# Attention, MLP and gate gradients on one core: dO sums one pair later, dwo and dw2 rows split between two engines, wide b and a products, four dV tiles stored in row pieces

## Chip, core and metric

The kernel runs on 1 core of one Trainium2 chip. The metric is device time in microseconds of one execution; lower is better. Three runs of the kernel before gave 405.79, 408.78 and 409.79 us (median 408.78).

## The reference

One decoding step of a gated mix of attention (A) and an MLP (B), and the gradients of all its inputs for a given `grad_out`. x has 640 elements, there are 32 heads of 128 with 4096 cached positions, and the MLP is 1728 wide. All tensors are bf16.

```python
def _A_ref(x, k_cache, v_cache, wq, wo):          # H, Dh = 32, 128
    q = (x @ wq).reshape(B, Sq, H, Dh).transpose(0, 2, 1, 3)
    scores = jnp.einsum("bhqd,bhkd->bhqk", q, k_cache) * (Dh ** -0.5)
    p = _softmax(scores, axis=-1)
    o = jnp.einsum("bhqk,bhkd->bhqd", p, v_cache)
    return o.transpose(0, 2, 1, 3).reshape(B, Sq, H * Dh) @ wo
def _B_ref(x, w1, b1, w2):
    h = jnp.einsum("bsd,df->bsf", x, w1) + b1
    sp = jnp.log1p(jnp.exp(-jnp.abs(h))) + jnp.where(h > 0, h, jnp.zeros_like(h))
    return jnp.einsum("bsf,fd->bsd", h * jnp.tanh(sp), w2)
g = _sigmoid((x * gate_w).sum(-1, keepdims=True))
out = g * _A_ref(...) + (1 - g) * _B_ref(...)
# returned: out and its gradients for A_x, A_k_cache, A_v_cache, A_wq, A_wo, B_w1, B_b1, B_w2, gate_w
```

The key and value caches are 33.6 MB each, and so are their gradients. With the weights and their gradients, 82.0 MB are read and 82.0 MB written.

## The kernel before, in words

The 32 heads go in 16 pairs. A pair's K or V is one tile of 128 partitions by 16 KB (2 MB): 64 partitions per head, 64 positions of 128 numbers in each. There are seven such buffers (`kv0` to `kv6`). A gradient tile is made in a buffer that its own K or V held, and stored from there, so a buffer comes free when its store has landed.

Each pair runs through 16 slots; (i, s) is slot s of pair i, and the order of all work is written out by hand. In slots 0 to 7 TensorE transposes V of pair i, in slots 8 to 15 K of pair i+1 (`transposes`, L368 to 376, with a ScalarE copy out of PSUM), and two slots later it forms dP or S from them (`products`, with 48 moving columns, W = 48, of which the first few count). The softmax is spread over slots 2 to 8 (`soft_max` to `soft_p`; `rz` is the reciprocal of its sum), o comes in slots 7 and 8, ds in 11, and the outer products dV in slots 9, 10, 12 and 13 and dK in slot 15 and in 0, 1 and 3 of the next pair (L463, 1.22 us each on VectorE).

Queues: loads are issued by SP, in the order of the list `loads` (L159 to 169). `pump` (L171) puts a load into SP's program as soon as that program has freed a buffer for it; SP then waits there until the store from that buffer has landed, and everything behind it on SP waits too. Stores of dV (slot 13) and dK (slot 3 of the next pair) are issued by POOL while loads remain, later by SP (L725 to 729, called at L757 and L776).

Heads also go in four groups of eight (g = 0 to 3, four pairs each). A group's rows of wo (1.3 MB) lie in `wob[g % 2]`, so groups 1 and 3 share a buffer, as do 0 and 2. What is done on it:

- `do_sum` (L287, VectorE, 8 per group): products of its rows with da, summed along the row: the gradient of o. It must be done before the group's first pair starts; `do_prep` builds dR, Dr and ndo from it in the slots behind.
- `a_cols` (L331, TensorE, 40 products per group with one moving column): the group's share of `a`.
- `dwo_row` (L352, ScalarE, 8 per group, 0.83 us each): overwrites the rows with the gradient of wo, behind `a_cols` and all the sums.
- `st_dwo` (L355, POOL) and, when it has landed, `ld_wo` (L156, SP) for the group two on.

For group g = 1 these stand at pair 8: `a_cols` in slots (8,2) to (8,4), `dwo_row` in (8,5) to (8,14), `st_dwo` at (9,0), `ld_wo(3)` at (9,1); `do_sum(3, 0)` stands at (10,6), `do_sum(3, 1)` at (10,14) and the other six at (11,5) to (11,7). Group 2's sums stand alike four pairs earlier, at (6,6), (6,14) and (7,5) to (7,7).

The MLP runs in pairs 0 to 6. Its w2 lies in 14 blocks of rows in columns of the wq tile: `mlp_b` (L566, TensorE, 70 products with one moving column, slots (1,14) to (2,2)) gives b, `mlp_dact` (L576, VectorE) reads the same blocks, and `mlp_dw2` (L581, ScalarE) overwrites them with the gradient of w2 in slots (2,3) to (3,6); `st_dw2` stores them at (3,9). `dx_sum` and `dwq_row` (L482, L487) do the like for wq, group by group.

Tables of the form `plan(i, {s: [(f, args)]})` and `at(i, s, f, args)` put such side work behind the main work of a slot (L647 to 703).

Of the kernel before, what the change touches and what calls it, by code (L numbers as in the profile page):

```python
# [9 lines left out]
ALU = mybir.AluOpType  # L10
AX = mybir.AxisListType
F32 = mybir.dt.float32
# [5 lines left out]
def kernel(  # L18
# [33 lines left out]
    nc = tc.nc  # L52
    P = 128
    _, H, Sk, Dh = A_k_cache.shape
# [5 lines left out]
    J = 64  # L60
    RC = D // P
# [4 lines left out]
    FN = FK + 1  # L66
    NBUF = 7
    NT = 4
    W = 48
# [32 lines left out]
    def C(shape, dt, name):  # L102
        return const.tile(shape, dt, name=name, tag=name)
# [3 lines left out]
    bufs = [big.tile([P, bufw.get(i, KVW)], BF16, name=f"kv{i}", tag=f"kv{i}") for i in range(NBUF)]  # L107
    wqa = big.tile([P, RC, H * Dh], BF16, name="wq", tag="wq")
    wob = [big.tile([P, 8, D], BF16, name=f"wo{i}", tag=f"wo{i}") for i in range(2)]
# [12 lines left out]
    kbuf, vbuf, mbuf = {}, {}, {}  # L122
# [48 lines left out]
    def pump():  # L171
        while loads and (free_q or not loads[0][0]):
            loads.popleft()[1]()
# [44 lines left out]
    mst = {}  # L218

    def misc(shape, dt, name):  # L220
        return one_ps.tile(shape, dt, name=name, tag="misc")
# [5 lines left out]
    db_bc = C([P, D], BF16, "db_bc")  # L227
    da_bc = C([P, D], BF16, "da_bc")
# [85 lines left out]
    a_acc = C([P, RC], F32, "a_acc")  # L314
    o8 = C([P, 8], BF16, "o8")
    o8f = C([P, 8], F32, "o8f")
# [13 lines left out]

    def a_cols(g, c0=0, c1=RC):  # L331
        if c0 == 0:
            mst["a"] = misc([P, RC], F32, "a_ps")
        ps = mst["a"]
        wv = wob[g % 2][:].rearrange("p k (n c) -> p k c n", c=RC)
        for c in range(c0, c1):
            for k in range(8):
                nc.tensor.matmul(ps[:, c:c + 1], lhsT=wv[:, k, c, :], rhs=o8[:, k:k + 1],  # L338
                                 start=(k == 0), stop=(k == 7))
        if c1 == RC:  # L340
            if g == 0:
                nc.vector.tensor_copy(a_acc[:], ps[:])
            else:
                nc.vector.tensor_tensor(a_acc[:], a_acc[:], ps[:], ALU.add)

    def scaled(eng, dst, src, col):
        if eng is nc.vector:
            nc.vector.tensor_scalar(dst, src, col, None, ALU.mult)
        else:
            nc.scalar.mul(dst, src, col)  # L350

    def dwo_row(g, k):  # L352
        nc.scalar.mul(wob[g % 2][:, k, :], da_bc[:], o8f[:, k:k + 1])  # L353

    def st_dwo(g, eng, k0=0, k1=8):  # L355
        eng.dma_start(dwo_v[g][:, k0:k1], wob[g % 2][:, k0:k1])
# [21 lines left out]
    def products(ps, src, c, col):  # L378
        for t in range(4):
            B = 4 * c + t  # L380
            for e in range(2):
                nc.tensor.matmul(ps[:, 4 * B:4 * B + W].rearrange("p (a b) -> p a b", b=4),  # L382
                                 lhsT=src[:, t, :, e],
                                 rhs=col[:, e, :, :].rearrange("p a b -> p (a b)").unsqueeze(1).to_broadcast([P, W // 4, 4]),
                                 start=(e == 0), stop=(e == 1))
# [116 lines left out]
    act_f = C([P, FN], F32, "act_f")  # L502
    act_b = C([P, FN], BF16, "act_b")
# [3 lines left out]
    b_acc = C([P, RC], F32, "b_acc")  # L507
# [5 lines left out]
    def w2row(k):  # L513
        n0 = HC + (k % 3) * D
        return wqa[0:P if k < FK else FR, k // 3, n0:n0 + D]

    def frange(k):
        return (P, slice(k, k + 1)) if k < FK else (FR, slice(FK, FN))
# [46 lines left out]

    def mlp_b(c0, c1):  # L566
        if c0 == 0:
            mst["b"] = misc([P, RC], F32, "b_ps")
        for c in range(c0, c1):
            for k in range(FN):  # L570
                n, ks = frange(k)
                nc.tensor.matmul(mst["b"][:, c:c + 1], lhsT=w2row(k).rearrange("p (n c) -> p c n", c=RC)[:, c, :], rhs=act_b[0:n, ks], start=(k == 0), stop=(k == FN - 1))
        if c1 == RC:
            nc.vector.tensor_copy(b_acc[:], mst["b"][:])

    def mlp_dact(k):  # L576
        n, ks = frange(k)
        nc.vector.scalar_tensor_tensor(junk[0:n, :], in0=w2row(k), scalar=1.0, in1=db_bc[0:n, :],  # L578
                                       op0=ALU.mult, op1=ALU.mult, accum_out=dact[0:n, ks])

    def mlp_dw2(k):  # L581
        n, ks = frange(k)
        nc.scalar.mul(w2row(k), db_bc[0:n, :], act_f[0:n, ks])

    def st_dw2():
        for t, v in w2_pieces:
# [30 lines left out]
    def at(i, s, f, *a):  # L617
        side.setdefault((i, s), []).append(lambda: f(*a))

    def plan(i, table):  # L620
        for s, tasks in table.items():
            for t in tasks:
                at(i, s, *t)

    def dx(g, part, c0, c1, *rcs):
        return [(dx_sum, g, part, c0, c1, rc) for rc in rcs]
# [4 lines left out]
    def rows(f, *ks):  # L631
        return [(f, k) for k in ks]

    def sums(g, *ks):
        return [(do_sum, g, k) for k in ks]

    def dwo(g, *ks):
        return [(dwo_row, g, k) for k in ks]

    def q_prep(i, s, g):  # L640
        plan(i, {s: [(q_half, g, 0)], s + 2: [(q_half, g, 1)], s + 3: [(q_dup, g)], s + 5: [(q_cols, g)]})

    def do_prep(i, s, g):
        plan(i, {s: [(do_hot, g)], s + 2: [(do_rows, g)], s + 3: [(do_dup, g)], s + 5: [(do_cols, g), (do_plain, g)]})
# [6 lines left out]
    for c, (i, s) in enumerate(((1, 14), (1, 15), (2, 0), (2, 1), (2, 2))):  # L651
        at(i, s, mlp_b, c, c + 1)
    plan(2, {5: rows(mlp_dact, 9, 10), 6: rows(mlp_dact, 11, 12), 7: rows(mlp_dact, 13), 14: sums(1, 0, 1)})
    q_prep(2, 8, 1)
    for k in range(FN):
        at(*((2, 3), (2, 4), (2, 6), (2, 7), (2, 9), (2, 10), (2, 12), (2, 13), (2, 14), (3, 1), (3, 2), (3, 3), (3, 4),
             (3, 6))[k], mlp_dw2, k)
    plan(3, {4: [(mlp_dh,)] + sums(1, 2), 5: sums(1, 3, 4), 6: sums(1, 5, 6), 7: sums(1, 7), 8: [(dh_hot, 0)],
             10: [(dh_row, 0)]})
    plan(3, {8: [(do_hot, 1)]})  # L660
    plan(3, {10: [(do_rows, 1)], 11: [(do_dup, 1)], 13: [(do_cols, 1), (do_plain, 1)], 14: [(dh_hot, 1)],
             15: [(o_dup, 0)]})
    plan(3, {9: [(st_dw2,)]})
    plan(4, {0: [(dh_row, 1)], 1: [(o_rows, 0)]})
    plan(4, {3: [(a_cols, 0, 0, 2)], 4: [(a_cols, 0, 2, 4)], 5: [(a_cols, 0, 4, 5)]})
    for k in range(8):
        at(4, (6, 7, 8, 9, 10, 12, 13, 14)[k], dwo_row, 0, k)
    plan(4, {5: rows(mlp_dxb, 0), 7: rows(mlp_dxb, 1), 14: rows(mlp_dxb, 2)})
    plan(5, {0: [(st_dwo, 0, nc.gpsimd)], 1: [(ld_wo, 2)], 5: rows(mlp_dxb, 3), 7: rows(mlp_dxb, 4), 14: dx(0, 0, 0, GC, 0)})
    plan(4, {10: [(ld_wq, HC, 2 * HC, nc.scalar)]})  # L670
# [2 lines left out]
    for g in range(NG - 1):  # L673
        i = 4 * g + 4
        if g:
            plan(i - 1, {14: [(o_dup, g)]})
            plan(i, {0: [(o_rows, g)], 2: [(a_cols, g, 0, 2)], 3: [(a_cols, g, 2, 4)], 4: [(a_cols, g, 4, 5)]})
            for k in range(8):
                at(i, (5, 6, 7, 9, 10, 12, 13, 14)[k], dwo_row, g, k)
            plan(i + 1, {0: [(st_dwo, g, nc.gpsimd)]})  # L680
            if g + 2 < NG:
                plan(i + 1, {1: [(ld_wo, g + 2)]})
        for k, (j, s) in enumerate((((1, 14), (2, 5), (2, 7), (3, 14), (3, 15)), ((1, 5), (1, 7), (2, 5), (2, 7), (2, 14)),
                                    ((0, 14), (1, 5), (1, 6), (1, 7), (1, 14)))[g]):
            if (g, k) != (0, 0):
                plan(i + j, {s: dx(g, g, 0, GC, k)})
            at(i + j, s + 1 if s < 15 else s, dwq_row, g, 0, GC, k)
    for g in (2, 3):
        i = 4 * g
        q_prep(i - 1, 2, g)  # L690
        plan(i - 2, {6: sums(g, 0), 14: sums(g, 1)})
        plan(i - 1, {5: sums(g, 2, 3), 6: sums(g, 4, 5), 7: sums(g, 6, 7)})
        do_prep(i - 1, 8, g)
    plan(12, {8: [(st_dwq, 0, HC, nc.scalar)]})
    plan(14, {6: [(st_dwq, HC, HC + GC, nc.gpsimd)]})
# [2 lines left out]
    g, i = NG - 1, NP - 2  # L698
# [14 lines left out]
    def run_products(i, s):  # L713
# [5 lines left out]
        else:  # L719
# [2 lines left out]
                S_ps[n] = one_ps.tile([P, 2 * J + W], F32, name="S", tag="S")  # L722
            products(S_ps[n], src, s - 8, qR[(n // 4) % 2][:, n % 4])

    def store_kv(dct, i, dst, eng):  # L725
        b = dct[i]
        eng.dma_start(dst, bufs[b][:, 0:J * Dh])  # L727
        free_q.append(b)
        pump()

# [3 lines left out]
    def slot(i, s):  # L734
# [16 lines left out]
        if chain_on:  # L751
            if s == 0:
                dq_row(i - 1)
            if s in (0, 1, 3):
                dk_quarter(i - 1, (0, 1, 3).index(s) + 1)
            if s == 3:
                store_kv(kbuf, i - 1, dKv[i - 1], nc.gpsimd if loads else nc.sync)  # L757
            if s == 2:
                soft_max(i)
            if s == 4:  # L760
                soft_maxt(i)
            if s == 7:
                soft_z(i)
# [9 lines left out]
        if s in (9, 10, 12, 13):  # L773
            outer(vbuf[i], st[i]["p"], Dr[(i // 4) % 2][:, i % 4, :], (9, 10, 12, 13).index(s))
            if s == 13:
                store_kv(vbuf, i, dVv[i], nc.gpsimd if loads else nc.sync)  # L776
# [73 lines left out]
    i, g = NP - 1, NG - 1  # L850
# [30 lines left out]
    dq_row(i)  # L881
    last_dv(1)
    a_cols(g)
    for k in range(8):
        dwo_row(g, k)
# [71 lines left out]
```

## Time and profile before

| What | us |
|---|---|
| three runs | 405.79, 408.78, 409.79 |
| span of the profiled execution, first to last instruction | 405.7 |
| busy: TensorE matmul / weight load | 299.9 / 275.3 |
| busy: VectorE / ScalarE / GpSimd | 279.1 / 259.9 / 25.1 |
| DMA: 164.88 MB, 15963 packets | mean 406 GB/s over the span |
| bytes read from and written to HBM | 82.03 MB and 82.03 MB |

The span is 0.1 us under the fastest run. How to read the rest of the profile: a row of instructions gives line, engine, operation, out<-in tiles and shapes, how many, busy time and the mean of one in ns, and the idle time of the engine ahead of them with what ended most of it. SPq, ACTq and POOLq are queues' own instructions (DMA issues and waits). The slices cut the span in 40 parts of 10.1 us, counted here from 0; a digit is a busy share in tenths, PEclk is the granted TensorE clock in tenths. From the DMA's issues: a 2 MB store by POOL landed 19.1 us after its issue at the median, a 2 MB load 18.8 to 18.9 us, a dwo store of 1.3 MB by POOL 26.2 us. The two forms of the products' rows: `b_ps` 70 with 128x1, first at 67.0 and last at 75.5 us; `a_ps` 160 with 128x1.

### The profile page before, as it was taken

To read this page: it belongs to the slowest core of one execution; us is meant where nothing else is said; L and a number is where in the kernel's file an instruction comes from. 1 tells how busy PE (TensorE), PEld (TensorE's weight loads), DVE (VectorE), ACT (ScalarE), POOL (GpSimd) and SP (SyncE) were. 2 spreads that over 40 slices of the span, in tenths; PEclk is the share of its full clock that TensorE was granted. 3 is DMA by queue.
4 is the path that set the end of the run, shared out by engine and by line. 5 is a ranking of instruction groups with operands and counts; after the bars stand their busy time and mean duration, and the time that the engine had idled before them with its cause. 6 is when DMAs were issued, how large, how long until landed. Compare 5 with 4: busy or idle time off the path is not lost.

```text
span 405.7 us, 13024 instructions
## 1 busy us (share of the span) xinstructions
PE 299.9 (74%) x5646; PEld 275.3 (68%) x5646; DVE 279.1 (69%) x596; ACT 259.9 (64%) x529; POOL 25.1 (6%) x50
## 2 busy tenths in 40 slices
PE   3769898998886887739979869704989998896210
PEld 3548898886775777729869769603889888886200
DVE  2744969489884968529795939306889598795850
ACT  3444545699857978617768976404676998986610
POOL 3000000002000101000000100000101010000020
PEclk9886999699999889857999999955999999999555
DMA  8999999999999999999999999999999999999993
GB/s 272 425 407 436 420 421 422 425 407 361 395 427 428 412 426 425 423 430 428 430 425 428 424 429 426 427 434 429 371 401 375 386 424 424 419 422 423 426 423 124
DMA packets 15963, 164.88 MB, mean 406 GB/s; under 512 B 1713, under 2 KB 1905, under 8 KB 6178
## 3 DMA queue, kind: packets, MB, share of 16 engines
q1 hardware_dynamic: 8832, 94.08, 55.9%
q0 software_dynamic: 5472, 63.42, 37.5%
q10 hardware_dynamic: 1602, 6.56, 4.0%
q8 instruction: 44, 0.72, 0.7%
q14 instruction: 13, 0.11, 0.1%
HBM read 82.03 MB, written 82.03 MB: 404 GB/s over the span
## 4 chain that ended last, share of the span: by engine, by line
issue 44%; DMA 22%; PE 13%; DVE 9%; ACT 4%; POOL 3%; SPq 0%; POOLq 0%; ACTq 0%; DVEq 0%
DMA kv<-in_A_k_cache_dram 11%; DMA out_dram<-wo 6%; DVE kv L463 5%; PE tr L372 5%; DMA wo<-in_A_wo_dram 5%; POOL out_dram L727 2%; ACT tch L375 2%; PE dq L431 2%; PE o L431 1%; PE dP L382 1%; PE S L382 1%; DVE wq L484 1%; ACT wq L350 1%; PE a_ps L338 1%; ACT wo L353 1%
## 5 line engine op out<-in xcount | busy, mean ns | idle before, releaser
L372 PE MATMUL tr<-idf,kv 128*128 128x128 f32 x1024 | 175.3, 298 | 13.6 <-DMA kv<-in_A_k_cache_dram 11.9
L375 ACT COPY tch<-tr 128x512 f32<-128x512 f32 x256 | 144.2, 586 | 57.1 <-PE tr L372 53.2
L372 PEld LDWEIGHTS tr<-idf,kv 128*128 128x128 f32 x1024 | 120.8, 153 | 19.7 <-issue 16.7
L382 PEld LDWEIGHTS <-tch 128*128 128x128 bf16 x2048 | 89.9, 100 | 57.4 <-ACT tch L375 52.5
L463 DVE TENSOR_TENSOR kv<-p_dup,Dr 128x2048 bf16<-128x2048 bf16 x64 | 76.6, 1220 | 5.5 <-ACT p_dup L422 5.2
L463 DVE TENSOR_TENSOR kv<-ds_dup,Qr 128x2048 bf16<-128x2048 bf16 x64 | 76.8, 1220 | 0.4
L382 PE MATMUL S<-qR,tch 128*128 128x48 bf16 x1024 | 48.4, 187 | 33.5 <-ACT tch L375 32.8
L431 PEld LDWEIGHTS <-kv 128*128 128x128 bf16 x2048 | 59.2, 97 | 4.6 <-issue 3.5
L382 PE MATMUL dP<-dR,tch 128*128 128x48 bf16 x1024 | 48.7, 187 | 10.6 <-ACT tch L375 10.0
L288 DVE SCALAR_TENSOR_TENSOR junk<-wo,da_bc 128x640 bf16<-128x640 bf16 x32 | 26.3, 822 | 33.2 <-DMA wo<-in_A_wo_dram 32.5
L431 PE MATMUL dq<-ds_m,kv 128*128 128x48 bf16 x1024 | 31.8, 184 | 4.1 <-DVE ds_m L453 2.5
L422 ACT ACTIVATE p_dup<-e_m,rz 64x128 bf16<-64x128 bf16 x32 | 12.7, 397 | 33.9 <-DVE rz L416 33.4
L727 POOL DMA_DIRECT2D out_dram<-kv x25 | 13.4, 536 | 296.5 <-DVE kv L463 244.4
L431 PE MATMUL o<-e_m,kv 128*128 128x48 bf16 x1024 | 31.6, 185 | 0.0
L353 ACT ACTIVATE wo<-da_bc,o8f 128x640 bf16<-128x640 bf16 x32 | 25.9, 826 | 1.6 <-PE a_ps L338 0.9
L350 ACT ACTIVATE wq<-dqrow,xf 128x1024 bf16<-128x1024 bf16 (+2 forms) x30 | 25.1, 860 | 1.4 <-DVE wq L484 1.0
L484 DVE SCALAR_TENSOR_TENSOR wq<-wq,dqrow 128x1024 bf16<-128x1024 bf16 (+2 forms) x30 | 25.1, 862 | 0.2
L437 DVE TENSOR_TENSOR o<-o,rz 128x2 f32<-128x2 f32 x16 | 2.5, 158 | 20.6 <-PE o L431 20.6
L404 DVE TENSOR_REDUCE negM<-mt 64x1 f32<-64x64 f32 x32 | 7.1, 222 | 11.4 <-PE mt L401 10.8
L457 ACT COPY ds_dup<-ds_m 64x128 bf16<-64x128 bf16 x32 | 9.5, 297 | 6.8 <-DVE ds_m L453 6.3
L409 ACT ACTIVATE e_m<-S,negM 64x64 bf16<-64x64 f32 x32 | 10.6, 331 | 4.5 <-DVE negM L404 4.0
L578 DVE SCALAR_TENSOR_TENSOR junk<-wq,db_bc 128x640 bf16<-128x640 bf16 (+1 forms) x14 | 11.5, 820 | 2.2 <-ACT db_bc L256 1.9
(159 smaller groups left out, 240.7 us busy)
## 6 DMA issues: line engine op xcount, KB each, us to landing
out_dram<-kv POOLq DMA_DIRECT2D x25, 2048.0 KB, 19.1
kv<-in_A_v_cache_dram SPq DMA_DIRECT2D x16, 2048.0 KB, 18.8
kv<-in_A_k_cache_dram SPq DMA_DIRECT2D x15, 2048.0 KB, 18.9
out_dram<-kv SPq DMA_DIRECT2D x5, 2048.0 KB, 25.5
wo<-in_A_wo_dram SPq DMA_DIRECT2D x4, 1280.0 KB, 19.8
out_dram<-kv SPq DMA_DIRECT2D x4, 1024.0 KB, 18.5
out_dram<-wo POOLq DMA_DIRECT2D x3, 1280.0 KB, 26.2
wq<-in_A_wq_dram SPq DMA_DIRECT2D x2, 1280.0 KB, 9.4
```

Source lines behind the costliest of these rows:

```text
L288: nc.vector.scalar_tensor_tensor(junk[:], in0=wob[g % 2][:, k, :], scalar=1.0, in1=da_bc[:], op0=ALU.mult, op1=ALU.mult, accum_out=do8[g % ...
L350: nc.scalar.mul(dst, src, col)
L353: nc.scalar.mul(wob[g % 2][:, k, :], da_bc[:], o8f[:, k:k + 1])
L372: nc.tensor.transpose(tp[:, t, :], src[:, 4 * c + t, :], idf[:])
L375: nc.scalar.copy(dst[:].rearrange("p a b e -> p (a b e)").bitcast(F32), tp[:].rearrange("p a b -> p (a b)"))
L382: nc.tensor.matmul(ps[:, 4 * B:4 * B + W].rearrange("p (a b) -> p a b", b=4), lhsT=src[:, t, :, e], rhs=col[:, e, :, :].rearrange("p a b - ...
L422: nc.scalar.activation(p[HS[hh]], e_m[i % 2][HS[hh], :, hh].unsqueeze(2).to_broadcast([64, J, 2]), ACT.Copy, scale=st[i]["rz"][HS[hh], hh: ...
L431: nc.tensor.matmul(st[i][key][:].rearrange("p (a b) -> p a b", b=2), lhsT=src[:, j, :], rhs=rhs[:, j, :].unsqueeze(1).to_broadcast([P, W / ...
L463: nc.vector.tensor_tensor(kview(b)[:, j0:j0 + n, :].rearrange("p j (a b) -> p j a b", b=2), col[:, j0:j0 + n, :].unsqueeze(2).to_broadcast ...
L484: nc.vector.scalar_tensor_tensor(w, in0=w, scalar=1.0, in1=dqrow[g % 2][:, c0:c1], op0=ALU.mult, op1=ALU.mult, accum_out=dq_acc[:, rc, par ...
L578: nc.vector.scalar_tensor_tensor(junk[0:n, :], in0=w2row(k), scalar=1.0, in1=db_bc[0:n, :], op0=ALU.mult, op1=ALU.mult, accum_out=dact[0:n ...
L727: eng.dma_start(dst, bufs[b][:, 0:J * Dh])
```

## The change

- The sums of groups 2 and 3 stand nine slots later for k = 0, at (6,15) and (10,15), and k = 1 at (7,4) and (11,4).
- `dwo_row` takes an engine. Group 1: all eight rows on VectorE in slots (8,5) and (8,6), its store at (8,7), the load of group 3's wo at (8,15). Group 0: four of the eight rows on VectorE. Groups 2 and 3: as before.
- `mlp_dw2` takes an engine: blocks 0 to 5 on VectorE at (2,3) and (2,4), 6 to 9 on ScalarE in (2,7) to (2,14), 10 to 13 on VectorE at (3,2). `st_dw2` stands at (3,4).
- The products of `mlp_b` and `a_cols` get 48 moving columns, copies of the one that counts; each overwrites the columns behind its own, which later products set anew.
- Two `dx_sum` and `dwq_row` of group 0 move from pair 7 to pair 6.
- The POOL stores of dV 3, 6, 9 and 12 are split by rows: 5+120+3, 14+105+9, 8+120 and 1+120+7, each piece a DMA of its own.

On VectorE the row is `tensor_scalar` by a column (`scaled`, L346, as it stands).

```diff
     def a_cols(g, c0=0, c1=RC):
         if c0 == 0:
-            mst["a"] = misc([P, RC], F32, "a_ps")
-        ps = mst["a"]
+            mst["a"] = misc([P, RC + W], F32, "a_ps")
+        ps = mst["a"][:, 0:RC]
...
-                nc.tensor.matmul(ps[:, c:c + 1], lhsT=wv[:, k, c, :], rhs=o8[:, k:k + 1],
+                nc.tensor.matmul(mst["a"][:, c:c + W], lhsT=wv[:, k, c, :], rhs=o8[:, k:k + 1].to_broadcast([P, W]),
                                  start=(k == 0), stop=(k == 7))
...
-    def dwo_row(g, k):
-        nc.scalar.mul(wob[g % 2][:, k, :], da_bc[:], o8f[:, k:k + 1])
+    def dwo_row(g, k, eng=nc.scalar):
+        scaled(eng, wob[g % 2][:, k, :], da_bc[:], o8f[:, k:k + 1])
...
-                nc.tensor.matmul(mst["b"][:, c:c + 1], lhsT=w2row(k).rearrange("p (n c) -> p c n", c=RC)[:, c, :], rhs=act_b[0:n, ks], start=(k == 0), stop=(k == FN - 1))
+                nc.tensor.matmul(mst["b"][:, c:c + W], lhsT=w2row(k).rearrange("p (n c) -> p c n", c=RC)[:, c, :],
+                                 rhs=act_b[0:n, ks].to_broadcast([n, W]), start=(k == 0), stop=(k == FN - 1))
...
-    def mlp_dw2(k):
+    def mlp_dw2(k, eng=nc.scalar):
         n, ks = frange(k)
-        nc.scalar.mul(w2row(k), db_bc[0:n, :], act_f[0:n, ks])
+        scaled(eng, w2row(k), db_bc[0:n, :], act_f[0:n, ks])
...
-    for k in range(FN):
-        at(*((2, 3), (2, 4), (2, 6), (2, 7), (2, 9), (2, 10), (2, 12), (2, 13), (2, 14), (3, 1), (3, 2), (3, 3), (3, 4),
-             (3, 6))[k], mlp_dw2, k)
+    for k in range(6):
+        at(2, 3 + k // 3, mlp_dw2, k, nc.vector)
+    for k, s in enumerate((7, 10, 13, 14)):
+        at(2, s, mlp_dw2, 6 + k)
+    for k in range(10, FN):
+        at(3, 2, mlp_dw2, k, nc.vector)
...
-    plan(3, {9: [(st_dw2,)]})
+    plan(3, {4: [(st_dw2,)]})
...
-        at(4, (6, 7, 8, 9, 10, 12, 13, 14)[k], dwo_row, 0, k)
+        at(4, (6, 7, 9, 10, 11, 11, 13, 14)[k], dwo_row, 0, k, nc.vector if k in (4, 5, 6, 7) else nc.scalar)
...
-            for k in range(8):
-                at(i, (5, 6, 7, 9, 10, 12, 13, 14)[k], dwo_row, g, k)
-            plan(i + 1, {0: [(st_dwo, g, nc.gpsimd)]})
             if g + 2 < NG:
-                plan(i + 1, {1: [(ld_wo, g + 2)]})
-        for k, (j, s) in enumerate((((1, 14), (2, 5), (2, 7), (3, 14), (3, 15)), ((1, 5), (1, 7), (2, 5), (2, 7), (2, 14)),
+                for k in range(8):
+                    at(i, 5 + k // 4, dwo_row, g, k, nc.vector)
+                plan(i, {7: [(st_dwo, g, nc.gpsimd)], 15: [(ld_wo, g + 2)]})
+            else:
+                for k in range(8):
+                    at(i, (5, 6, 7, 9, 10, 12, 13, 14)[k], dwo_row, g, k)
+                plan(i + 1, {0: [(st_dwo, g, nc.gpsimd)]})
+        for k, (j, s) in enumerate((((1, 14), (2, 5), (2, 6), (2, 7), (2, 14)), ((1, 5), (1, 7), (2, 5), (2, 7), (2, 14)),
                                     ((0, 14), (1, 5), (1, 6), (1, 7), (1, 14)))[g]):
...
-        plan(i - 2, {6: sums(g, 0), 14: sums(g, 1)})
-        plan(i - 1, {5: sums(g, 2, 3), 6: sums(g, 4, 5), 7: sums(g, 6, 7)})
+        plan(i - 2, {15: sums(g, 0)})
+        plan(i - 1, {4: sums(g, 1), 5: sums(g, 2, 3), 6: sums(g, 4, 5), 7: sums(g, 6, 7)})
...
+    uneven = {3: (5, 120, 3), 6: (14, 105, 9), 9: (8, 120), 12: (1, 120, 7)}
+
     def store_kv(dct, i, dst, eng):
         b = dct[i]
-        eng.dma_start(dst, bufs[b][:, 0:J * Dh])
+        p0 = 0
+        for n in uneven.get(i, (P,)) if dct is vbuf and eng is nc.gpsimd else (P,):
+            eng.dma_start(dst[p0:p0 + n], bufs[b][p0:p0 + n, 0:J * Dh])
+            p0 += n
         free_q.append(b)
         pump()
```

More of the change, by code (lines that the diff above doesn't have):

```diff
@@ L341, in a_cols @@
             if g == 0:
-                nc.vector.tensor_copy(a_acc[:], ps[:])
+                nc.vector.tensor_copy(a_acc[:], ps)
             else:
-                nc.vector.tensor_tensor(a_acc[:], a_acc[:], ps[:], ALU.add)
+                nc.vector.tensor_tensor(a_acc[:], a_acc[:], ps, ALU.add)
     def scaled(eng, dst, src, col):
@@ L567, in mlp_b @@
         if c0 == 0:
-            mst["b"] = misc([P, RC], F32, "b_ps")
+            mst["b"] = misc([P, RC + W], F32, "b_ps")
         for c in range(c0, c1):
@@ L571, in mlp_b @@
                 n, ks = frange(k)
-                nc.tensor.matmul(mst["b"][:, c:c + 1], lhsT=w2row(k).rearrange("p (n c) -> p c n", c=RC)[:, c, :], rhs=act_b[0:n, ks], start=(k == 0), stop=(k == FN - 1))
+                nc.tensor.matmul(mst["b"][:, c:c + W], lhsT=w2row(k).rearrange("p (n c) -> p c n", c=RC)[:, c, :],
+                                 rhs=act_b[0:n, ks].to_broadcast([n, W]), start=(k == 0), stop=(k == FN - 1))
         if c1 == RC:
-            nc.vector.tensor_copy(b_acc[:], mst["b"][:])
+            nc.vector.tensor_copy(b_acc[:], mst["b"][:, 0:RC])
     def mlp_dact(k):
```

## Prediction, on record ahead of the result

> **What bounds the kernel now.** First the page's slices: does one resource run full from end to end?
>
> ```profile
> PEclk9886999699999889857999999955999999999555
> DMA  8999999999999999999999999999999999999993
> GB/s 272 425 407 436 420 421 422 425 407 361 395 427 428 412 426 425 423 430 428 430 425 428 424 429 426 427 434 429 371 401 375 386 424 424 419 422 423 426 423 124
> ```
>
> The DMA engines do: 425 to 430 GB/s in nearly every slice, while no engine passes 74% of the span. So time comes only from the slices below that rate: the first, slices 9 and 10 (361, 395), slices 28 to 31 (371 to 401) and the last. Then who starves the DMA there: busy time by stretches, whose last columns are granted PE clock, DMA share and GB/s.
>
> ```profile
> core 0: us, PE busy (x) PEld busy (x) DVE busy (x) ACT busy (x) POOL busy (x), PEclk, DMA share, GB/s
> 67.00:80.00 13.00, 12.09 (x180) 11.40 (x176) 7.75 (x16) 5.78 (x13) 1.06 (x2) 0.74 1.00 425
> 91.00:100.00 9.00, 7.88 (x142) 6.74 (x140) 8.46 (x17) 8.95 (x18) 1.39 (x3) 1.00 0.93 354
> 100.00:113.00 13.00, 10.19 (x212) 9.18 (x213) 11.57 (x26) 10.17 (x24) 1.84 (x4) 1.00 1.01 398
> ...
> 257.00:277.00 20.00, 4.10 (x102) 3.76 (x102) 0.00 (x0) 1.98 (x3) 0.00 (x0) 0.71 1.01 431
> 277.00:285.00 8.00, 5.25 (x66) 4.93 (x67) 7.74 (x16) 5.63 (x11) 0.00 (x0) 0.50 0.95 404
> 285.00:300.00 15.00, 14.22 (x268) 12.54 (x266) 12.22 (x26) 10.20 (x25) 1.06 (x2) 0.97 0.98 387
> 300.00:325.00 25.00, 23.06 (x487) 21.74 (x486) 19.67 (x41) 19.65 (x41) 1.06 (x2) 1.00 0.98 385
> 325.00:345.00 20.00, 17.90 (x385) 16.43 (x381) 18.52 (x32) 18.28 (x36) 1.06 (x2) 1.00 1.02 428
> 394.00:405.70 11.70, 0.00 (x0) 0.00 (x0) 0.00 (x0) 0.00 (x0) 0.52 (x2) 0.50 0.39 163
> ```
>
> From 257 to 277 VectorE does nothing; the DMA lives on its queue, then lacks work from 277 to 325. At 91 to 113 ScalarE (99%) and VectorE (94%) are full and the stores come late. The waits and the chain name the cause of the hole:
>
> ```profile
> DVE junk L288 <- DMA wo<-in_A_wo_dram: 32.5, 2, 20.2
> ACT p_dup L422 <- DVE rz L416: 33.4, 5, 19.3
> ```
>
> ```profile
> 231.62 26.36 DMA out_dram<-wo
> 258.04 19.07 DMA wo<-in_A_wo_dram
> 277.13 0.83 DVE junk L288 x2
> ```
>
> The first dO sum of group 3 waits 20.2 us for its wo tile, whose load waits for the store of group 1's dwo from that buffer. The other wait (12.3 us, 168 to 180) starves nothing: 428 GB/s there.
>
> **The change, part by part.** Durations are those of the profiled execution: span 405.7 us, 0.1 under the fastest of the three runs (405.79) and 3.1 under their median; I carry the 3.1 over.
>
> *Group 1's store earlier, group 3's sums later.* All 8 dwo rows go to VectorE in slots (8,5) and (8,6), the store to (8,7), ahead of dV 8 on POOL's queue. No VectorE instruction of the before multiplies a 128x640 tile by a column; bounds are the 128x1024 COPY of L259, 0.43 us, and the two-input product L288, 0.82 us. I take 0.35, scaled from the copy, the nearer one (one tensor in, both bf16): 8 x 0.35 = 2.8 us (6.6 at most). VectorE idled 1.9 us before rz and 2.1 behind it there (218.3 to 222.5), so up to 1 us (2.6) reaches the pair, in a stage where compute follows the loads closely. The store is issued near 221.5 instead of 231.62; with its old 26.4 us it lands by 248. On SP the wo load stays between the load that dV 8 frees and the next one. That earlier load went at 249.9 and waits for dV 8, now behind 1.3 MB: 3.1 us at 428. So wo goes out at 250 to 253 and lands (19.1) at 269 to 272, not 277.1. Group 3's first sum moves from (10,6) to (10,15), nine slots: from 277.1 to 286.7 in the before, so from 256.9 to about 266. The wait left is 3 to 6 us instead of 20.2, and dV 10 (285.19, 8.1 us behind the wait) now stands ahead of it, near 265. What is late next is the V load for pair 11 (269.2 in the before), so compute paces with loads again. Loss recoverable, against 428: 8 x (1-404/428) + 15 x (1-387/428) + 25 x (1-385/428) = 0.4+1.4+2.5 = 4.4 us. Pair 11 still carries both preparations of group 3 and took 22.1 us (dV 10 to dV 11) where the DMA needs 20, so I take 3.5. Behind the waiting sum on VectorE stand the dK quarters and dq of pair 10: the 3 to 6 us reach them. Group 2's sums move alike: their 12.3 us shrink to about 2, worth nothing under a full DMA.
>
> *Wide b and a.* Between 70.9 and 77.7 the granted clock was 0.5 though PE was 93% busy, and the 70 b products with one moving column lie there. Transposes took 1.04 to 1.12 us per four instead of 0.64, S and dP products 0.53 instead of 0.36: 4 x 0.46 + 3 x 0.17 = 2.3 us on PE, which bound that stretch (ScalarE waits for transposes). The wide form is priced by L382: 8 with 48 columns in 0.36 us against 14 narrow ones in 0.79, no dearer. Bounds 0 and -2.3; I take -2.3, since 48-column products run at full clock all over the trace. The Trainium skill (TensorE: Matmul & The Clock Gate, Part 1) has the gate close after an idle window of about 3.4 us and says that it does not count instructions; by that rule a 93% busy PE would not be throttled for narrow columns, and widening gives 0. The trace speaks against the rule as stated, not for the cure.
>
> *dw2 and dwo rows.* Ten dw2 rows leave ScalarE (0.845 each), five of them due past (2,9), where ScalarE is full; VectorE gets four at (3,2): 1.4 us (3.3). Net for the stores of 91 to 113: 2.3 from the clock and about 1 from ScalarE earlier, minus 1.4. Loss there: 9 x (1-354/428) + 13 x (1-398/428) = 2.5 us; I take 1.5 (0 to 2.5). The dw2 store stands between the same two kv stores on POOL, with its rows done sooner. Four dwo rows of group 0 and two dx sums moved from pair 7 to 6 lie under a full DMA: nothing; uncovered, the rows would cost 1.4 and the sums 2.4.
>
> *Stores in pieces.* The semaphore arrivals of the last store (issued 387.43) show 15 engines done by 400.7 and one at 404.3; of the one before, 398.2 and 401.9. One engine is 3.6 us behind at the end, in stretches from 285 on up to 5. A 16 KB row took 0.611 us. The large pieces leave one engine out of 15 + 1: up to 31 rows fewer for it if it is always the same (some 25 if small pieces give some back), about 15 us, and 25/15 x 0.611 = 1.0 us more for each other. If it is the late one: -3.6+1.0 = -2.6; if not: +1.0. The trace shows no engine numbers. I take -2.6, since a relief of 15 us is far over the lag and dV 12 (325.3) lies where the lag stands and dV 9 (250.2) just ahead of it. Seven more issues of 0.53 us on a POOL 94% idle: nothing. The Trainium skill (DMA: Bandwidth & Descriptors, How many engines (k)) gives a piece the largest divisor up to 16, on consecutive engines from a rotating cursor, but some copies ceil(rows/16) per engine from engine 0. By the first one engine is spared throughout; by the second the last is, and engine 0 gets the extra rows of rival (a).
>
> Sum: 405.7 - 3.5 - 1.5 - 2.6 = 398.1; with 3.1: **401.2 us**.
>
> **Rivals.** (a) The spared engine is not the late one: -3.5-1.5+1.0 = -4.0, 404.8; the missing numbers speak for it. If small pieces start from the first engine each time, it gets 2+1+1+2 = 6 rows more, 6 x 0.611 = 3.7 us; were it the late one, 407.5. (b) The hole only moves: wo lands behind the displaced dV 8, pair 11 stays slower than the loads, and the tail keeps its late engine: 0 to -2, about 407.5. For it: the queue covered all but 4.4 of 20 us before. Against: dV 10 now leaves 20 us earlier. (c) Slower: the 105-row piece of dV 6 does not spread. 105 rows on one engine take 64 us, and dV 6 (issued 188.04, landed 208.9) frees the buffer of the load that SP issued at 209.00; all later loads queue behind it. Some 43 us late, less about 18 us of queued stores: near 430. It decides from about 20 rows per engine (12 us against 4.9). Against: a 64-row store in the before completed with its neighbours. (d) All recoverable loss returns, 4.4+2.5+3.6 = 10.5, near 398.
>
> **Numbers.** Forecast 0.53 (its own range 398 to 405), (a) 0.20, (b) 0.12, (c) 0.08, (d) 0.07. What a measurement of this kernel tells from no change is about 1%, 404.7. Faster: nearly all of the forecast (0.50), 0.09 of (a), (d) = 0.66; within: the rest of (a), (b), a little of the forecast = 0.25; slower: (c) and a bad edge of (b) = 0.09. Range 396 to 408: from (d) with the fastest run to (b).
>
> **What would show it.** The wait of L288 for wo falls from 32.5 to under 10 us and the dwo store of group 1 is issued near 222; GB/s stays over 415 from 277 to 325 and over 400 from 91 to 113; no 0.5 clock near 71 to 78; new VectorE rows of 0.3 to 0.45 us at L349; the last arrivals within 1.5 us of each other. Wrong if a wait of over 10 us on VectorE remains near 266, if the split stores take over 30 us to land, or if the last store still has one arrival 3 us late.

## Result, and the profile after

The changed kernel takes 418.56 us (median of four runs, 414.43 to 419.50) beside 408.50 for the kernel before: 1.0239 times as long, 95% interval 1.0200 to 1.0278. Forecast were 401.2 us and faster. The profiled execution has a span of 416.0 us. In the table of runs below, medians are over all runs, while the ratios leave out a run that took over 1.5% more than the fastest of its kernel (one each in e2, e5 and e14).

The same slices as for the kernel before (TensorE clock, DMA share, GB/s; 40 slices, here of 10.4 us):

```profile
PEclk9879999998999869977999898685799999989655
DMA  8999999999999999999999999999999999999991
GB/s 272 423 410 431 425 411 428 425 426 421 421 429 364 395 426 424 429 430 425 421 421 419 423 429 403 314 388 421 337 410 355 415 376 369 405 425 423 407 418 62
```

Slices 9 and 10 are mended (421, 421, against 361 and 395). But there are new holes at slice 12 (364), 25 (314) and 28 to 33 (337, 355, 376, 369), while the DMA engines stay busy all the time (9 throughout). Busy and yet slow: that is not a DMA that lacks work, but one whose transfers take longer. The kernel before was in part the same. The prediction's own lines have a DMA share of 0.98 at 387 and 385 GB/s from 285 to 325, and the 918 rows of 16 KB that start there average 0.664 us, against 0.615 from 150 to 250. (918 x 0.053 / 16 = 3.0 us of DMA time over 0.611 a row, of the 3.9 us that the prediction counts as lost there.) So "lacks work from 277 to 325" holds for the smaller part only: from 310 to 320 fifteen packets or more are in flight throughout, at 370 and 331 GB/s. Whole tiles can be slow as well. Busy time by stretches, in the columns of the same view of before:

```profile
core 0: us, PE busy (x) PEld busy (x) DVE busy (x) ACT busy (x) POOL busy (x), PEclk, DMA share, GB/s
67.00:80.00 13.00, 11.72 (x232) 11.00 (x231) 9.89 (x25) 6.98 (x15) 0.53 (x1) 1.00 1.02 435
91.00:100.00 9.00, 7.18 (x124) 6.89 (x122) 8.72 (x21) 5.49 (x14) 2.38 (x4) 0.87 1.01 424
100.00:113.00 13.00, 11.05 (x219) 9.92 (x218) 12.40 (x24) 8.55 (x19) 1.55 (x3) 0.96 1.00 421
...
260.00:265.00 5.00, 2.67 (x45) 2.64 (x46) 0.43 (x2) 2.81 (x6) 0.00 (x0) 0.65 1.00 328
265.00:270.00 5.00, 5.00 (x62) 4.84 (x62) 3.53 (x9) 2.48 (x6) 0.00 (x0) 0.67 0.99 287
```

From 260 to 270, when the two pieces of dV 9 are moved (issued 247.66 and 248.17, landed 273.1 and 284.7), the DMA is 99 to 100% busy at 328 and 287 GB/s. Its packets show it: between 265 and 270 the 49 rows of 16 KB on POOL's queue average 1.131 us, the 35 on SP's queue 0.611 as ever.

The waits, the chain that ended last and the new rows:

```profile
DVE junk L288 <- DMA wo<-in_A_wo_dram: 16.4, 1, 16.4
```

```profile
261.61 29.14 DMA wo<-in_A_wo_dram
290.77 0.83 DVE junk L288 x2
```

```profile
L348 DVE TENSOR_SCALAR wo<-da_bc,o8f 128x640 bf16<-128x640 bf16 x12 | 3.8, 382 | 0.0
L572 PE MATMUL b_ps<-act_b,wq 128*128 128x48 bf16 x65 | 3.4, 198 | 0.5 <-DMA wq<-in_A_wq_dram 0.5
```

VectorE still waits 16.4 us for group 3's wo, which lands at 290.7 instead of 277.1: its load went out at 261.61, right behind the load for which SP waited until dV 8 had landed (227.82 to 261.0). The wide b products take 0.198 us each, and the stretch at half clock (67 to 80) is at 1.00.

### The profile page after: what moved, and what is told of

It reads as the page before. It is cut to its first block, busy times and chain, and to the rows that moved or that the text cites. A ratio compares the mean times of both kernels' runs of the same rounds, so it can differ in the third digit from the quotient of the medians.

```text
span 416.0 us, 13036 instructions
## 1 busy us (share of the span) xinstructions
PE 299.8 (72%) x5643; PEld 277.6 (67%) x5646; DVE 285.7 (69%) x618; ACT 247.0 (59%) x507; POOL 28.8 (7%) x57
## 4 chain that ended last, share of the span: by engine, by line
DMA 42%; issue 19%; PE 19%; DVE 12%; ACT 4%; POOL 1%; SPq 1%; ACTq 0%; POOLq 0%; DVEq 0%
DMA out_dram<-kv 15%; DMA kv<-in_A_k_cache_dram 15%; PE tr L372 7%; DMA wo<-in_A_wo_dram 7%; DVE kv L463 7%; DMA kv<-in_A_v_cache_dram 4%; PE o L431 2%; PE dP L382 2%; PE dq L431 2%; PE S L382 1%; PE a_ps L338 1%; ACT tch L375 1%; PE q_ps L275 1%; DVE wq L484 1%; DVE junk L288 1%
## 5 line engine op out<-in xcount | busy, mean ns | idle before, releaser
L382 PEld LDWEIGHTS <-tch 128*128 128x128 bf16 x2048 | 91.6, 100 | 22.6 <-ACT tch L375 16.5
L738 POOL DMA_DIRECT2D out_dram<-kv x32 | 17.1, 535 | 304.0 <-DVE kv L463 291.2
L288 DVE SCALAR_TENSOR_TENSOR junk<-wo,da_bc 128x640 bf16<-128x640 bf16 x32 | 26.3, 822 | 17.1 <-DMA wo<-in_A_wo_dram 16.4
L396 DVE TENSOR_REDUCE m<-S 64x1 f32<-64x64 f32 x32 | 7.0, 220 | 17.3 <-PE S L382 17.1
L350 ACT ACTIVATE wo<-da_bc,o8f 128x640 bf16<-128x640 bf16 x20 | 15.9, 825 | 1.5 <-PE a_ps L338 1.0
L478 PE MATMUL dqr_ps<-idb,dqb 128*128 128x128 bf16 x32 | 5.0, 245 | 13.7 <-DVE dqb L475 13.7
```

The source lines that it names most:

```text
L288: nc.vector.scalar_tensor_tensor(junk[:], in0=wob[g % 2][:, k, :], scalar=1.0, in1=da_bc[:], op0=ALU.mult, op1=ALU.mult, accum_out=do8[g % ...
L738: eng.dma_start(dst[p0:p0 + n], bufs[b][p0:p0 + n, 0:J * Dh])
```

## Experiments

All in one table first; "before" is the kernel before, measured beside each run.

| Run | What it is | us, median (runs) | before | ratio, 95% |
|---|---|---|---|---|
| e1_whole | change, whole stores | 407.16 (10) | 407.83 | 0.9974, 0.9951 to 0.9997 |
| e2_pieces_alone | before + the pieces | 417.55 (4) | 407.83 | 1.0204, 1.0131 to 1.0277 |
| e3_112_16 | change, 112+16 rows | 419.43 (4) | 407.83 | 1.027, 1.022 to 1.032 |
| e4_columns | change, two column halves | 408.89 (10) | 407.83 | 1.0035, 1.0015 to 1.0056 |
| e5_64_64 | change, 64+64 rows | 419.85 (4) | 408.02 | 1.0254, 1.0203 to 1.0305 |
| e12_even_odd | change, even + odd rows | 407.58 (10) | 407.79 | 0.9997, 0.9977 to 1.0018 |
| e11_loads_64_64 | whole stores, four V loads 64+64 | 419.66 (4) | 407.52 | 1.0283, 1.0256 to 1.0310 |
| e6_hole_alone | before + group 1's store and the later sums | 407.68 (12) | 408.02 | 1.0000, 0.9982 to 1.0017 |
| e7_wide_alone | the rest, whole stores | 408.10 (12) | 408.02 | 1.0005, 0.9987 to 1.0023 |
| e8_wo_earlier | e1 with the wo load at (8,8) | 408.04 (12) | 408.02 | 1.0006, 0.9988 to 1.0023 |
| e9_tail_120_8 | e6, last four stores 120+8 rows | 412.48 (6) | 407.52 | 1.0114, 1.0090 to 1.0139 |
| e10_stores_by_act | e6, K and V stores by ScalarE's queue | 410.56 (8) | 407.52 | 1.0079, 1.0051 to 1.0107 |
| e13_loads_60_60_8 | whole stores, two V loads 60+60+8 | 412.88 (5) | 407.90 | 1.0130, 1.0106 to 1.0154 |
| e14_stores_60_60_8 | change, two dV stores 60+60+8 | 413.64 (6) | 407.90 | 1.0138, 1.0084 to 1.0192 |

### Which part costs: the pieces

e1 takes the pieces out of the change, e2 puts them alone into the kernel before.

```diff
-    uneven = {3: (5, 120, 3), 6: (14, 105, 9), 9: (8, 120), 12: (1, 120, 7)}
+    uneven = {}
```

> The changed kernel with its four dV tiles stored whole. Theory P (the pieces cost the time): 399 to 405 us, 3 to 5% under the changed kernel's 418.6, and no 16 KB store row over 0.7 us on average in any stretch. Rival M (the moved sums, rows and store cost it): 414 or more, the same as with pieces.

> The kernel before with only the four split stores. Theory P: 413 to 420 us, store rows of over 1 us behind each split store. Rival M: 407 to 410, as the kernel before.

The pieces carry the whole loss: without them it is gone, and alone they cost 0.0204 x 407.83 = 8.3 us. In e1 a hole at the old place is mostly filled again:

```profile
GB/s 280 423 415 431 412 426 424 394 425 371 421 433 423 410 400 423 425 430 435 426 421 431 428 424 427 430 419 432 435 402 414 415 417 420 413 430 421 407 401 35
```

Slices 24 to 33 sum to 4211 here and to 3788 with the pieces; the difference of 423 GB/s over slices of 10.4 us is 4.4 MB, which a DMA at 428 moves in 10.3 us. So most of the lost time lies between 250 and 354, from the pieces of dV 9 on; how much of it the slow rows take themselves, and how much the late wo tile, is not separated. Slice 9 is at 371 here, against 421 with the pieces, so the stretch behind 91 is not mended in every version. (Neither did e1 reach the 399 to 405 that was expected; see below.)

### What of the pieces costs

A piece can cost because an engine is left out, because there are more DMAs, or because its rows lie otherwise on the engines.

```diff
+    uneven = {i: (112, 16) for i in (3, 6, 9, 12)}                                              # e3; in e4 and e5 (64, 64)
...
-            eng.dma_start(dst[p0:p0 + n], bufs[b][p0:p0 + n, 0:J * Dh])                         # e3, e5: by rows
+            eng.dma_start(dst[:, p0 * 64:(p0 + n) * 64], bufs[b][:, p0 * 64:(p0 + n) * 64])     # e4: all rows, half the columns
```

> The changed kernel with the four tiles stored as 112 + 16 rows: every engine gets 7 + 1 rows, none is left out, but the rows lie otherwise on the engines than in a whole store. If the loss is from where a piece's rows lie (theory A): 412 to 420. If it is from leaving one engine out of 16 and loading the others unevenly (theory U): 399 to 405, as with whole stores.

> The changed kernel with the four tiles stored as two halves of the columns: two DMAs and two landings for each, all 128 rows in both, 8 KB a row. If the loss is from the number of DMAs and landings on POOL's queue (theory N): 410 to 420. By theories A and U: 399 to 405.

> The changed kernel with each of the four dV tiles stored as 64 + 64 rows: two pieces, all 16 engines in both, 4 + 4 rows each. A (a piece cut by rows puts its rows on other engines than a whole 128-row transfer does, and they then get in each other's way): 412 to 424, and 16 KB store rows well over 0.611 us behind each of the four stores. U (only pieces whose rows do not divide evenly over 16 engines, 7 + 1 or 15 engines, are dear): 405 to 409, near the 407.2 of the version with whole stores.

With 112+16 or 64+64 rows, numbers that divide evenly by 16, the loss is as large as with the change's own pieces: U falls in both. Two column halves, as many DMAs, take 408.89 us. That lies between the ranges of N and of A and U, so all three missed the time; but they cost at most 0.6% over the kernel before and 1.7 us over whole stores (407.16), where the cuts by rows cost 2.5 to 2.7%. So N falls as the cause of the loss: it is the cut by rows. Is it a matter of POOL's queue? e11 leaves the stores whole and cuts four loads on SP's queue:

```diff
+                for r in (slice(0, 64), slice(64, P)) if dct is vbuf and i in (3, 6, 9, 12) else (slice(0, P),):
+                    nc.sync.dma_start(bufs[b][r, t * n:(t + 1) * n], src[r, t * n:(t + 1) * n])
```

> The changed kernel with whole stores, and the loads of V 3, 6, 9 and 12 by SP as 64 + 64 rows each. A in general (any transfer cut by rows puts its rows on other engines, and these get in each other's way): 411 to 422, as the stores in 64 + 64 rows cost, with 16 KB load rows over 0.611 us where the pieces run. Q (only stores on POOL's queue suffer): 405.5 to 409.

It costs as much, so Q falls. And it shows slow rows without a store beside them: between 70 and 75 only SP's queue moves data, the last rows of K 3 and then the lower half of V 3 (issued at 67.36).

```profile
core 0: us, PE busy (x) PEld busy (x) DVE busy (x) ACT busy (x) POOL busy (x), PEclk, DMA share, GB/s
65.00:70.00 5.00, 5.00 (x127) 4.88 (x126) 4.94 (x8) 2.88 (x7) 0.53 (x1) 1.00 1.02 435
70.00:75.00 5.00, 4.10 (x79) 3.86 (x77) 3.69 (x6) 2.03 (x4) 0.00 (x0) 1.00 1.16 239
```

Sixteen packets or more are in flight throughout, at 239 GB/s, 0.55 of the 435 just before; the 73 rows that start there (by count the last 47 of K 3 and the first 26 of the half) average 1.267 us, 2.07 times 0.611. So about half the rate is left while a half of the partitions is filled. That agrees with the Trainium skill (SBUF — State Buffer, Door 1: The DMA port swizzle, and "Can I just issue two DMAs to hit both halves?"): partitions 0 to 63 reach only 8 of 16 ports, and two DMAs on the two halves do not add up. It is no proof: K 3's rows lie on all partitions and are slow too, and no run here moves a half alone. If the ports are the cause, halves that each spread over all partitions should be free:

```diff
-            eng.dma_start(dst[p0:p0 + n], bufs[b][p0:p0 + n, 0:J * Dh])
+            r = slice(0, P) if n == P else slice(p0 // 64, P, 2)
+            eng.dma_start(dst[r], bufs[b][r, 0:J * Dh])
```

> The changed kernel with each of the four dV tiles stored as its 64 even and its 64 odd rows, in place of the lower and the upper 64. P (a piece is slow because its rows lie in one half of the partitions, and spreading them over all 128 cures it): 406 to 410. R (any piece cut by rows gives its rows to other engines than a whole transfer does, and that alone costs): 412 to 423, as 64 + 64 did. The Trainium skill (SBUF — State Buffer, Door 1: The DMA port swizzle) has partitions 0 to 63 reach 8 of 16 ports and a range over all 128 all 16; by that P, unless engines in step still meet at one port.

They are: 407.58 us, against 419.85 with the lower and upper halves. The stretch that ran at 328 and 287 in the changed kernel:

```profile
core 0: us, PE busy (x) PEld busy (x) DVE busy (x) ACT busy (x) POOL busy (x), PEclk, DMA share, GB/s
260.00:265.00 5.00, 4.07 (x90) 3.92 (x89) 4.94 (x9) 3.78 (x8) 0.00 (x0) 1.00 0.99 419
265.00:270.00 5.00, 2.37 (x61) 2.24 (x60) 2.79 (x4) 2.32 (x3) 0.53 (x1) 0.97 1.01 429
```

### Why a filled hole pays nothing

e6 is the kernel before with group 1's eight rows on VectorE, its store at (8,7), the load of wo at (8,15) and the later sums; e7 is the rest of the change with whole stores. e8 moves one load of e1:

```diff
-                plan(i, {7: [(st_dwo, g, nc.gpsimd)], 15: [(ld_wo, g + 2)]})
+                plan(i, {7: [(st_dwo, g, nc.gpsimd)], 8: [(ld_wo, g + 2)]})
```

> The kernel before with group 1's eight dwo rows on VectorE, its store at (8,7), the load of group 3's wo at (8,15) and the sums of groups 2 and 3 nine slots later; nothing else. H (the prediction's term: a filled hole shortens the kernel): -3.5 us, some 404. E (the end is set by one DMA engine that is behind the others and busy throughout, so the hole's return goes to the 15 others): within 0.5% of before, 406.5 to 409, although GB/s between 277 and 325 rises over 415.

> The kernel before with the rest of the change but the stores in pieces: 48-column b and a products, dw2 rows and four dwo rows of group 0 on VectorE, two dx sums one pair earlier. H (the prediction's term): -1.5 us, some 406. E (one late DMA engine sets the end): within 0.5% of before, 406.5 to 409; the granted clock stays at 1.0 through the b products under both.

> The changed kernel with whole stores and with the load of group 3's wo at slot (8,8) instead of (8,15), so that on SP it stands ahead of the load that waits for dV 8. Its issue should come right behind the landing of group 1's dwo store, near 249 instead of 259.5, and VectorE's wait of 12.9 us at the first sum of group 3 should fall under 4. H (what is left of the hole costs time): 1 to 3 us under the version with whole stores (407.2), so 404 to 406. E (one late DMA engine sets the end): 406 to 408.5, the wait gone and nothing gained.

In time E holds in all three; its mechanism shows in e6. There the hole of 277 to 325 is filled, and the kernel is not a microsecond faster:

```profile
core 0: us, PE busy (x) PEld busy (x) DVE busy (x) ACT busy (x) POOL busy (x), PEclk, DMA share, GB/s
277.00:285.00 8.00, 3.52 (x28) 2.94 (x30) 4.75 (x8) 1.54 (x3) 0.00 (x0) 0.50 1.01 434
285.00:300.00 15.00, 13.80 (x250) 12.07 (x248) 11.81 (x30) 10.39 (x26) 0.53 (x1) 0.98 1.01 429
300.00:325.00 25.00, 22.86 (x481) 21.32 (x480) 19.69 (x37) 21.14 (x44) 2.13 (x4) 1.00 1.01 420
...
395.00:400.00 5.00, 0.00 (x0) 0.00 (x0) 0.00 (x0) 0.00 (x0) 0.00 (x0) 0.50 0.19 78
400.00:404.90 4.90, 0.00 (x0) 0.00 (x0) 0.00 (x0) 0.00 (x0) 0.00 (x0) 0.50 0.04 17
```

Against 404, 387 and 385 GB/s before; the 16 KB rows from 285 to 325 average 0.621 us, against 0.664. What comes back is seen at the end, in the kernel before:

```profile
395.00:400.00 5.00, 0.00 (x0) 0.00 (x0) 0.00 (x0) 0.00 (x0) 0.00 (x0) 0.50 0.68 278
400.00:405.70 5.70, 0.00 (x0) 0.00 (x0) 0.00 (x0) 0.00 (x0) 0.00 (x0) 0.50 0.04 17
```

The last ten microseconds carry 278 x 5.0 + 17 x 5.7 = 1.49 MB before and 78 x 5.0 + 17 x 4.9 = 0.47 MB in e6. So 1.0 MB (2.4 us at 428) did move earlier; but in both kernels one engine out of 16 works on to the end, at a share of 0.04. The arrivals of the last store:

| | issued | 15 engines by | the last |
|---|---|---|---|
| before | 387.43 | 400.7 | 404.3 |
| e6_hole_alone | 387.31 | 397.6 | 403.5 |
| e1_whole | 387.95 | 398.1 | 404.5 |
| e8_wo_earlier | 389.49 | 399.7 | 406.6 |
| changed kernel | 398.84 | 409.1 | 414.7 |

In e6 fifteen engines are 3 us earlier, the last one only 0.8. The loads tell the same: in e6 those of V 13, K 14, V 14 and K 15 go out 5.6, 5.7, 4.9 and 5.2 us earlier than before, and land at 320.2, 331.9, 342.8 and 351.9, later than before (313.7, 324.8, 337.5, 348.6), because their last arrival is now 7.3 to 8.5 us behind the second-last, against 4.4, 0.2, 0.5 and 0.7. The lag has also changed places: in the kernel before, the stores by POOL that landed from 309 to 345 had it (3.8 to 5.1 us), in e6 those from 316 to 340 had 0.2 to 1.1 and the loads had it. So compute gets its tiles no sooner, and issues the last store at the same moment.

In e7 this is seen less well. Its stores that land from 208 to 252 have their median arrival 1.0 to 1.2 us earlier than before and their last one 1.3 to 1.5 us later, which fits a late engine; but the hole behind 277 is still open, and at the end fifteen engines are done by 400.8 and the last at 405.1, no earlier than before. In e8 even the wait is gone,

```profile
L288 DVE SCALAR_TENSOR_TENSOR junk<-wo,da_bc 128x640 bf16<-128x640 bf16 x32 | 26.3, 821 | 0.8
```

and the time is 408.04. But the wo load that now goes first holds up those behind it: V 12 goes out at 279.73, in e1 at 275.14, and fifteen engines have landed V 14 by 338.1, in e1 by 334.8. So e8 tells what the move is worth, and not that a late engine ate the return.

### The late engine

Can it be relieved, and what makes it late? e9 cuts the last four stores, on SP's queue; e10 takes the K and V stores off POOL's queue:

```diff
+            for r in (slice(0, 120), slice(120, P)):                           # e9, the last dV and dK halves
+                nc.sync.dma_start(dKv[i][r, h], bufs[fb][r, h])
...
+                    at(i, 5, store_kv, kbuf, i - 1, dKv[i - 1], nc.scalar)     # e10; dV at (i, 15)
```

> The version with the filled hole alone (e6_hole_alone, 407.7), with the last four stores (two halves each of dV 15 and dK 15, 8 KB rows, issued by SP) as 120 + 8 rows. In that version's profile the last store had 15 arrivals by 397.6 and one at 403.5. L (one DMA engine that is behind sets the end, and it is the one that a 120-row store on 15 engines leaves out): it loses 4 x 8 rows x 0.309 us = 9.9 us, the others get at most 4 rows more, so the last arrival comes near 399 and the time is 402 to 405. M (the late engine is another one, or the pieces slow each other down as in the changed kernel): 407 to 411, one arrival still 5 us behind the second-last. The Trainium skill (DMA: Bandwidth & Descriptors, Latency and other measured facts) calls engines 7 and 15 usually slower than the rest, and its paragraph on the number of engines puts a piece of 120 rows issued by SP on engines 0 to 14; by these two L would hold if 15 is the late one here.

> The version with the filled hole alone, with the K and V gradient stores issued by ScalarE's queue two slots later instead of POOL's queue (the dwo, dw2, dw1 and dwq stores stay on POOL). S (POOL's queue makes one engine late): the gap of the last store's last arrival behind its second-last falls from 5.9 to under 2 us and the time to 400 to 404. F (the engine is late for another cause, such as the instruction fetches): the gap stays at 4 to 7 us and the time at 406 to 412, the upper part for waits of ScalarE behind VectorE. The Trainium skill (DMA: Bandwidth & Descriptors, Latency and other measured facts) guesses that the slower engines come from the descriptor rings of stores issued by GpSimd; by that S.

e9 was no clean test: its pieces slow each other (8 KB rows 0.40 to 0.53 us instead of 0.309), and SP could issue the last two only at 402. e10 tells more, though not as it seems at the end, where the last arrivals lie within 0.5 us. Until 346 the gap was there as ever (4.9 us at 286, 8.4 at 331, 7.1 at 340), with the K and V stores on another queue. Then the load of V 15 waited until 358.52 for a store of which one engine still had rows to move:

```profile
core 0: us, PE busy (x) PEld busy (x) DVE busy (x) ACT busy (x) POOL busy (x), PEclk, DMA share, GB/s
340.00:350.00 10.00, 8.72 (x182) 8.29 (x181) 7.76 (x17) 9.01 (x20) 0.85 (x1) 1.00 0.95 395
350.00:358.50 8.50, 6.48 (x149) 6.13 (x147) 8.37 (x17) 6.75 (x13) 0.00 (x0) 1.00 0.15 56
```

Fifteen engines idle for some 7 us (352.2 to 359.5), the late one catches up, and the time goes to 410.56: the same debt, as it seems, paid at another place. So F holds up to 346, though not in the gap at the end: the K and V stores on POOL's queue are not what makes the engine late. The Trainium skill (DMA: Bandwidth & Descriptors, Latency and other measured facts) calls two engines usually slower and guesses at the descriptors of GpSimd's stores; one late engine is seen here, and the guess is not supported for it, though the smaller stores stayed on POOL's queue. Nor do the instruction fetches explain it alone: the one at 355.4, taken while only the late engine moved data, left its 16 KB rows back to back.

The last two runs cut pieces of 60 rows that lie all over the partitions; by their number they are meant to leave one engine out:

```diff
+                for r in (slice(0, 120, 2), slice(1, 120, 2), slice(120, P)) if dct is vbuf and i in (11, 14) else (slice(0, P),):  # e13; e14: dV 9 and 12
```

> The changed kernel with whole stores, and the loads of V 11 and V 14 as 60 even rows, 60 odd rows and the last 8, by SP: one engine gets 16 rows fewer (9.8 us at 0.611), the others about one more. L (one late engine sets the end, and it is the one left out): the last store's last arrival, 6.4 us behind the second-last with whole stores, comes within 3 us, and the time falls by 2 to 5 us to 402 to 405. M (it is another engine): 406 to 409, the gap as it was. The Trainium skill (DMA: Bandwidth & Descriptors, How many engines (k), and Latency and other measured facts) has such a piece on the first 15 engines and calls 7 and 15 the slower ones; by that L if 15 is the later of the two.

> The changed kernel with whole stores but for dV 9 and dV 12, which POOL issues as 60 even rows, 60 odd rows and the last 8. Each 60-row piece leaves out one engine. L (it leaves out the late one): 402 to 405. M (the engine left out is another one, or changes from piece to piece): 406 to 409, no loss as even and odd rows gave none (407.6), and one arrival still some 6 us behind at the end.

Both theories missed the time. These pieces cost again, 1.3 and 1.4% for two tiles; between 270 and 275 in e13 42 load rows average 0.863 us. From 265 to 270, while the first 60 rows were still on their way (landed 269.44), 46 load rows average 0.749 and POOL's 56 store rows, of whole tiles, 0.714; so the last 8 rows, which lie side by side, are not the only cause, and the pieces slow other transfers too. A spread over the partitions is not enough; the halves that cost nothing were 64 even and 64 odd rows. On the question itself: in e13 the last arrival is still 6.8 us behind the second-last, so the engine that 60 rows are meant to leave out on SP's queue is probably not the late one (the slow pieces blur this). In e14 the gap falls to 0.2 us, but there the second-last is 6.9 us behind the median: two engines are late instead of one. Which engine is late, and why, stays open. So does why some cuts by rows are slow and others not.

## Why the prediction was wrong

- **Stores in pieces, -2.6 us: the step that failed.** They cost 8.3 us alone (5.3 to 11.3 by the interval). The step counted rows per engine and priced each at the 0.611 us of a whole tile's row; its bounds, -2.6 and +1.0, both rest on that. On POOL's queue rows then averaged up to 1.131 us, 1.85 times that. The trace of before had no piece of a 128-row tile beside other transfers, and the 64-row store that "completed with its neighbours" showed that it spread over engines, not what its rows cost. That the large pieces leave one engine out is shown by no run, since the trace has no engine numbers, and the relief did not show either: the changed kernel's last arrival is 5.6 us behind the second-last, more than the 3.6 before.
- **Rival (c), slower, 0.08.** Its sign was right, its mechanism was not: the load behind dV 6 went out 6.2 us later than before (215.2), not some 43, at 410 GB/s or more from 180 to 230, and the loss lies elsewhere. Pieces landed in 8.7 to 36.6 us, where 105 rows on one engine alone would take 64. So the sign was luck.
- **Group 1's store earlier, -3.5 us.** Alone 0 (-0.7 to +0.7). The mechanism ran as described: store issued at 222.22 in e6 (forecast 221.5), 277 to 325 at 420 to 434 GB/s. What failed is "loss recoverable, against 428": it counts the mean of 16 engines as idle time to be had back, while three quarters of it from 285 to 325 were slow rows, and the time is that of the engine behind. The prediction knew the lag of 3.6 us and used it only for the pieces. Within this term the landing of wo was mis-sized: forecast 269 to 272 with a wait of 3 to 6 us, measured 280.2 and 9.1 in e6, 281.9 and 12.9 in e1, 290.7 and 16.4 in the changed kernel. The load of V 11 ahead of it on SP waited for dV 8, which took 27.8 to 33.2 us behind the dwo store, and so went out at 257.7 to 261.2, not at 250 to 253.
- **Wide products and dw2 rows, -1.5 us.** The mechanism was right: full clock at 67 to 80, 424 and 421 GB/s from 91 to 113 (forecast over 400). e7 alone gives 0 (-0.5 to +0.9), as the hole does; that a late engine is the reason here too is only in part seen. In e1 the second half of the range stays at 427 from 100 to 113, but 91 to 100 is at 370. The row on VectorE takes 0.382 us, forecast 0.35.
- **The signs named** for "wrong" all came: a VectorE wait over 10 us (16.4, until 290.7), split stores over 30 us (34.3 to 36.6 for three of the five pieces of dV 6 and dV 9), one last arrival over 3 us late (5.6). Of the signs for "right", the early dwo store (219.85), over 400 GB/s from 91 to 113, the full clock and the 0.382 us rows came; the wait of L288 under 10 us and over 415 GB/s from 277 to 325 (411, 375 and 380) did not. Rival (b) was right for e1, the version without the pieces, in its mechanism too (wo behind the displaced dV 8, the tail keeps its late engine): 407.16 against 407.5.

## What to carry to other kernels

Cut a 128-partition transfer by columns or leave it whole; where it must be cut by rows, try 64 even and 64 odd rows, the one such cut that cost nothing here, and price a piece by a row of such a piece, not of a whole tile. Read a dip in GB/s beside the DMA share: a share of 0.98 at 387 GB/s is slow transfers, not idle engines. Before a hole in the DMA's mean rate is priced, look at the sixteen arrivals of the last transfers: if one of them is always late, a filled hole can be worth nothing, as in e6. That relieving the late engine would pay is not shown: the runs that tried lost time on their pieces. A stage that looks mended in GB/s proves nothing until the last arrival moves.

## What was not expected of the hardware

- The end of a whole tile and the first rows of a half of 64 neighbouring partitions moved at 239 GB/s with 16 packets or more in flight, against 435 just before; 64 even and 64 odd rows cost nothing (ratio 0.9997), 60 even, 60 odd and 8 cost 1.3 to 1.4%.
- Slow rows can keep to the queue that holds the pieces (265 to 270 in the changed kernel: POOL's 1.131 us on average, SP's 0.611) or spread to the other (295 to 300: 99 rows on SP's queue, which has no pieces, at 0.800). Whole tiles alone have them too (kernel before, 315 to 320: 77 load rows at 0.798).
- One of 16 DMA engines ends 3.6 to 6.9 us behind the second-last in the kernel before, e1, e6 and e8. In e6 POOL's stores show it falling back from 1.5 us at 258 to 5.3 at 294, at a DMA share of 1.01 (277 to 300).
